# Scores of a chunked linear attention computed below the diagonal only, in quarters of the TensorE array

## The chip, the cores and the metric

The kernel runs on one core of one Trainium2 chip. The metric is the device time of one execution in microseconds (us); lower is better. TensorE is called PE below, its weight loads PEld; VectorE is DVE, ScalarE ACT, GpSimd POOL, and SyncE, which here only issues DMAs, SP.

## What is computed

A linear attention with decay (RWKV-5) runs over 4 batches, 8 heads, 768 tokens and head size 48, and its output is routed to one of 8 experts (3072 tokens of width 384, hidden width 1024):

```python
for t in range(S):
    cur = einsum('bhd,bhe->bhde', u[None] * k[:, :, t], v[:, :, t])
    y[:, :, t] = einsum('bhd,bhde->bhe', r[:, :, t], state + cur)
    state = w[None, :, :, None] * state + einsum('bhd,bhe->bhde', k[:, :, t], v[:, :, t])
...
e = argmax(x @ w_gate);  out = gate * (relu(x @ w1[e]) @ w2[e])
```

Everything is float32. Cut into chunks of 128 tokens, the attention of one chunk is a 128x128 matrix of scores between the chunk's own tokens (strictly later tokens see earlier ones, with the decay; a token sees itself through u), applied to v, plus the state of all earlier chunks.

## The kernel before

**Stages.** The attention takes 16 pairs of heads (U = 16, four pairs to each of four batches), each of 6 chunks of C = 128 tokens. Two heads of 48 channels lie in one tile, at partitions 0 to 47 and 64 to 111; 48 to 63 are zero rows that are loaded with r and k. After the attention the tokens, sent to a table of rows in HBM by indirect DMA from POOL (`send`, L410), are read back expert by expert, and two dense layers follow; that stage is not touched.

**One pair.** The loop over pairs is at L732, and the order on every engine is the order of the calls there. For pair i: PE forms the products of each token with itself, `p_own` (L279), from `rp` = r*k, which POOL's `pairs` (L270) made; DVE turns them (`own_t`, L288). PE forms the scores, `p_scores` (L291): for 6 chunks and 2 heads one product of 48 rows, 128 weight columns and 128 moving columns, the whole 128x128 square. The two heads lie in two row halves of the array. ACT writes 12 scaled identity matrices into the tile A (`diag`, L300: 12 activations), the diagonal of the scores. DVE copies the scores over it where a mask, `strict`, says so (`mask`, L305: 3 copies, which leave out what is on and above the diagonal). PE then does `p_tr(i-2)` (L356: output turned, and gate logits), `p_ds(i)` (L315: the chunks' state increments from `Kd`), and `p_out(i-1)` (L329: A times v at L340, state times r at L345). DVE's `scan` (L323) runs the state over the chunks. ACT's `keep` (L361) and `out_t` (L348) empty PSUM. DVE's `scale` (L264) multiplies r and k by decays for pair i+1, POOL's `pairs(i+1)` and `keys(i+1)` (L274, `Kd` = k times decay, one instruction of 128x480) follow; for i in 7, 8, 11, 12 `keys` goes to DVE.

**Order.** On POOL each pair begins with a copy of one element, `turn` (L744), that waits for `own_t(i)`, and so holds back `pairs(i+1)`. Once in four pairs (i = 6, 10, 14) comes the rank of the previous batch's tokens (`p_rank`, `slots`, `gates`), and once (i = 5, 9, 13) the choice of experts, `choose` (L368, six short DVE instructions). The `send`s stand at the end of a pair on POOL: one for i = 6, two for i = 7 and 8, one for i = 9, and so on. For i = 7, 11 and 15 the scores of chunks 4 and 5 come after `p_ds`. In pairs 6, 10 and 14 `mask(i, 2)` stands ahead of `keep(i-2)`.

**Start.** Before the loop: PE runs 17 filling products (L121) while the first loads arrive; the decays are made on POOL and DVE (L141); `key_decay` and `p_key_decay` (L156, L160) make the table T3 that `keys` needs: DVE product, 4 PE transposes, 2 ACT copies. Then pair 0's steps, 8 more filling products on yps[0] (L730), and pair 1.

**Data.** The first three r, k loads and all later ones are one DMA of 112 partitions (L94). v and k lie token by token in vk, chunk by chunk.

Of the kernel before, what the change touches and what calls it, by code (L numbers as in the profile page):

```python
# [40 lines left out]
def bc(ap, shape):  # L41
    return ap.to_broadcast(shape)


def straight(tc, rk, vk, w, w1, w2, out, flag):
# [45 lines left out]
    def load_rk(i):  # L91
        if i < U:
            b, hp = divmod(i, HP)
            nc.sync.dma_start(rks[i % 3][0:KP], rk[b, hp].rearrange("h p u s -> (h p) u s")[0:KP])  # L94

    def load_vk(i):
        if i < U:
# [9 lines left out]
    def p_fill(n, o):  # L107

        for _ in range(n):
            nc.tensor.matmul(o, lhsT=ident, rhs=ident, start=True, stop=True, skip_group_check=True)  # L110
# [4 lines left out]
    def clear():  # L115
# [2 lines left out]
        nc.sync.dma_start(rows.rearrange("(e n) c -> e (n c)", e=E)[:, PAD * HP * Q:CAP * HP * Q].rearrange(  # L118
            "e (p z) -> p e z", p=128), bc(zt[:, None, :], [128, E, nz]))

    p_fill(17, X01[1][:, 0, :])  # L121
    strict = cp.tile([128, C], FP32, name="strict")
    nc.gpsimd.memset(strict, 1.0)
    nc.gpsimd.affine_select(out=strict, in_=strict, pattern=[[1, C]], base=-1, channel_multiplier=-1,
                            compare_op=ALU.is_ge, fill=0.0)

    pw = cp.tile([KP, 8, HP], FP32, name="pw")
    nc.vector.tensor_scalar(out=pw[:, 0, :], in0=wt, scalar1=W_LO, scalar2=W_HI, op0=ALU.max, op1=ALU.min)
# [1 line left out]
    TTf = TT.rearrange("p a u c -> p (a u c)")  # L130
    inv = cp.tile([KP, HP], FP32, name="inv")

    T3c = cp.tile([KP, HP, C], FP32, name="T3c")
    T3 = cp.tile([128, HP, 2 * D], FP32, name="T3")

    def two(h0, nh, first, second, n):

# [16 lines left out]
                                bc(inv[:, h0:h0 + nh, None, None], [KP, nh, 2, m]), op=ALU.mult)  # L154

    def key_decay(h0, nh):  # L156
        nc.vector.tensor_tensor(T3c[:, h0:h0 + nh, :], TT[:, h0:h0 + nh, 1, :],
                                bc(pw[:, 7, h0:h0 + nh, None], [KP, nh, C]), op=ALU.mult)

    def p_key_decay(h0, nh):  # L160
        for hp in range(h0, h0 + nh):
            nc.tensor.transpose(tr[:, hp * 128:hp * 128 + KP], T3c[:, hp, :], ident[0:KP, 0:KP])
        nc.scalar.copy(T3[:, h0:h0 + nh].rearrange("p a (h d) -> p a h d", h=2),
                       tr[:, h0 * 128:(h0 + nh) * 128].rearrange("p (a h d) -> p a h d", a=nh, h=2)[:, :, :, 0:D])


    dec = cp.tile([KP, HP, D, G - 1], FP32, name="dec")
# [22 lines left out]
        nc.scalar.copy(sel[:, :, :, 2 * D:], wgs)  # L190

    def numbers():
        nc.gpsimd.tensor_copy(tri, strict)
        nc.gpsimd.memset(ones, 1.0)
        nc.gpsimd.iota(it[:, 0:E], pattern=[[-1, E]], base=E, channel_multiplier=0)
        nc.gpsimd.tensor_copy(rev, it[:, 0:E])
        nc.gpsimd.iota(it[:, E:2 * E], pattern=[[N // 128, E]], base=0, channel_multiplier=0)
        nc.gpsimd.tensor_copy(osum, it[:, E:2 * E])
# [61 lines left out]
    def place(c, h):  # L260

        return c + 4 * h if c < 4 else 8 + 2 * h + c - 4
# [10 lines left out]

    def keys(i, eng=None):  # L274
        hp, v = i % HP, vks[i % 4]
        (eng or nc.gpsimd).tensor_tensor(Kds[i % 2], v[:, G:2 * G - 1, :], bc(T3[:, hp, None, :], [128, G - 1, 2 * D]),
                                         op=ALU.mult)

    def p_own(i):  # L279


        hp = i % HP
        x = rps[i % 2][0:KP].rearrange("p (c a j) -> p a c j", a=4, j=32)
        for a in range(4):
            nc.tensor.matmul(dsb[32 * a:32 * a + 2, 240:240 + 32 * G].rearrange("p (c j) -> p c j", j=32),
                             lhsT=ubs[:, hp, :], rhs=x[:, a], start=True, stop=True, skip_group_check=True)

    def own_t(i):  # L288
        nc.vector.transpose(own[i % 2].rearrange("p c m -> p (c m)"), dsb[:, 240:240 + 32 * G])  # L289

    def p_scores(i, cs):  # L291
        r = RKs[i % 3]
        for c in cs:
            for h in range(2):
                q = slice(64 * h, 64 * h + D)
                o = X01[h][:, c, :] if c < 4 else X23[:, h, (c - 4) * C:(c - 3) * C]
                nc.tensor.matmul(o, lhsT=r[q, 1, c * C:(c + 1) * C], rhs=r[q, 0, c * C:(c + 1) * C],  # L297
                                 start=True, stop=True, skip_group_check=True)

    def diag(i):  # L300
        A = Aw[i % 2]
        for c, h in [(c, 0) for c in range(4)] + [(c, 1) for c in range(4)] + [(c, h) for h in range(2) for c in (4, 5)]:
            nc.scalar.activation(A[:, place(c, h), :], ident, func=ACT.Copy, scale=own[i % 2][:, c, h:h + 1])  # L303

    def mask(i, k):  # L305
        A = Aw[i % 2]
        m = strict.bitcast(I32)
        if k < 2:
            nc.vector.copy_predicated(A[:, 4 * k:4 * k + 4, :], bc(m[:, None, :], [128, 4, C]), X01[k])  # L309
        else:  # L310
            nc.vector.copy_predicated(A[:, 8:12, :].rearrange("p (h c) t -> p h c t", h=2),
                                      bc(m[:, None, None, :], [128, 2, 2, C]),
                                      X23[:, :, 0:2 * C].rearrange("p h (c t) -> p h c t", c=2))

    def p_ds(i):  # L315
        v = vks[i % 4]
# [640 lines left out]
def general(tc, rk, vk, w, w1, w2, out):  # L957
# [117 lines left out]
    def load_pair(b, hp):  # L1075
        i = b * HP + hp
        kT, rT = kTs[i % 2], rTs[i % 2]
        for hi in range(2):
            q = slice(64 * hi, 64 * hi + D)
            nc.sync.dma_start(rT[q, :], rk[b, hp, hi, 0:D, 0])  # L1080
            nc.sync.dma_start(kT[q, :], rk[b, hp, hi, 0:D, 1])
        vt = ap2.tile([128, G, 2 * D], FP32, name="vt")
        nc.sync.dma_start(vt, vk[b, hp][:, 0:G, :])
        return kT, rT, vt

    def half(b, hp, hf, kT, rT, vt, St, xb):
# [330 lines left out]
def _layout(inputs):  # L1417


    import numpy as _np  # L1420
    x = {k: _np.asarray(v) for k, v in inputs.items()}
    r, k, v = (x[n].reshape(B, HP, 2, S, D) for n in "rkv")
    rk = _np.zeros((B, HP, 2, 64, 2, S), _np.float32)
    rk[:, :, :, 0:D, 0] = r.transpose(0, 1, 2, 4, 3)
    rk[:, :, :, 0:D, 1] = k.transpose(0, 1, 2, 4, 3)
    vk = _np.concatenate([a.reshape(B, HP, 2, G, C, D).transpose(0, 1, 4, 3, 2, 5).reshape(B, HP, C, G, 2 * D)[:, :, :, :n]
                          for a, n in ((v, G), (k, G - 1))], axis=3)
    w = _np.ones((KP, HP), _np.float32)
# [34 lines left out]
```

## Time and profile before

| | us |
|---|---|
| median of 3 runs | 372.37 (370.84 to 372.86) |
| the profiled execution, its own time | 367.2 |
| its span | 365.3 |
| attention: pair 2's `p_own` to the first expert product (L479) | 20.0 to 110.2 |
| one pair in that stretch, `p_own` to `p_own` | 6.22; 6.62 with the rank; 6.55 with split scores |
| busy in the span: PE, DVE, POOL, ACT | 353.3, 261.5, 204.6, 142.7 |

The profile is one execution, so sums below are made against its span and then carried to the median. A row of instruction groups gives line, engine, operation, output and inputs with their shapes, count, total busy time, the mean of one in ns, and the idle time before them with its releaser. The timeline gives start, duration, engine, line, operation. In the chain of waits (the work that ended last, followed back from the end) each piece has start, length and name; the chain passes through PE almost without a break from 20.0 us on. [...] PE counts are twice the calls: x24 is 12 products. Two DMAs bring a pair: 672 KB of r, k and 528 KB of vk; from 10 to 60 us the 16 DMA engines are 93% busy or more.

### The profile page before, as it was taken

The page shows a single profiled execution, that of the slowest core. Times are in us where ns is not written, and L with a number is a line of the kernel's source. Part 1 is how long each engine was busy: PE and PEld are TensorE (multiplying, and loading weights), DVE is VectorE, ACT ScalarE, POOL GpSimd, SP SyncE. Part 2 cuts the span into 40 slices and gives each one's busy share as a digit, 9 for nine tenths or more (in the row PEclk, how much of TensorE's full clock was granted, in tenths as well). Part 3 has the DMA queues.
Part 4 walks back from the last instruction along what each step waited for, and adds up shares of the span by engine and source line. Part 5 has one row for each costly group of instructions (what it writes and reads, how often), then busy time and mean ns, then how long its engine had stood idle before and what let it go on. Part 6 is the DMA issues. An engine that isn't in the chain of part 4 may idle for free.

```text
span 365.3 us, 9077 instructions
## 1 busy us (share of the span) xinstructions
PE 353.3 (97%) x3355; PEld 335.1 (92%) x3355; DVE 261.5 (72%) x653; ACT 142.7 (39%) x411; POOL 204.6 (56%) x242
## 2 busy tenths in 40 slices
PE   8999999999999999999999999999999999999991
PEld 8788888878889999999999999999999999999891
DVE  6988798887872258675797994896788688685531
ACT  2688787777784301323213312312221231122210
POOL 5389889898864521642107308805912941999341
PEclk9999999999999999999999999999999999999998
DMA  7999999986566974988358237525842943313301
GB/s 211 272 253 241 282 255 264 255 249 195 212 170 203 316 282 99 245 257 217 126 178 196 88 92 200 159 86 168 191 129 93 210 148 127 102 51 108 126 20 50
DMA packets 35205, 65.08 MB, mean 178 GB/s; under 512 B 18617, under 2 KB 19657, under 8 KB 35152
## 3 DMA queue, kind: packets, MB, share of 16 engines
q1 hardware_dynamic: 29648, 49.86, 50.3%
q0 software_dynamic: 3776, 9.84, 7.6%
q10 hardware_dynamic: 1728, 4.72, 3.7%
q8 instruction: 28, 0.46, 0.6%
q14 instruction: 25, 0.20, 0.2%
HBM read 53.29 MB, written 11.40 MB: 177 GB/s over the span
## 4 chain that ended last, share of the span: by engine, by line
PE 90%; DVE 2%; POOL 2%; issue 2%; DMA 1%; POOLq 0%; ACT 0%; DVEq 0%
PE X L501 12%; PE X L563 10%; PE X L479 8%; PE tr L603 7%; PE yps L603 7%; PE X L297 6%; PE yps L340 6%; PE yps L501 5%; PE tr L358 5%; PE yps L345 3%; PE tr L501 3%; PE dsb L501 3%; PE dsb L603 3%; PE yps L563 2%; PE dsb L320 2%
## 5 line engine op out<-in xcount | busy, mean ns | idle before, releaser
L675 POOL DMA_INDIRECT out_dram<-yo,ix x28 | 28.4, 1013 | 68.0 <-DVE ia L592 63.8
L303 ACT ACTIVATE A<-ident,own 128x128 f32<-128x128 f32 x192 | 57.9, 390 | 7.0 <-DVE own L289 6.6
L412 POOL DMA_INDIRECT rows<-xb,slot x24 | 30.3, 1262 | 12.0 <-issue 4.8
L563 PE MATMUL X<-hT,w2s 128*128 128x160 f32 (+5 forms) x288 | 36.5, 287 | 0.0
L563 PEld LDWEIGHTS X<-hT,w2s 128*128 128x128 f32 x288 | 36.2, 191 | 0.2
L603 PE MATMUL yps<-tums,sums 128*128 128x192 f32 x184 | 32.4, 326 | 0.0
L603 PEld LDWEIGHTS yps<-tums,sums 128*128 128x128 f32 x184 | 30.3, 190 | 0.0
L675 POOL DMA_INDIRECT out_dram<-yt,it x16 | 16.8, 1048 | 22.1 <-DVE so L621 10.9
L272 POOL TENSOR_TENSOR rp<-rk 112x768 f32<-112x768 f32 x15 | 28.8, 1919 | 0.0
L266 DVE TENSOR_TENSOR RK<-rk,TT 112x1536 f32<-112x1536 f32 x16 | 27.8, 1735 | 1.1 <-DMA rk<-in_rk_dram 0.9
L297 PEld LDWEIGHTS X<-RK 48*128 48x128 f32 x384 | 23.1, 187 | 5.3 <-issue 4.3
L297 PE MATMUL X<-RK 48*128 48x128 f32 x384 | 27.1, 283 | 0.2 <-DVE RK L266 0.2
L309 DVE COPY_PREDICATED A<-strict,X 128x512 f32<-128x512 int32 x32 | 23.3, 742 | 5.0 <-ACT A L303 4.9
L501 PE MATMUL X<-xT,w1s 128*128 128x208 f32 (+5 forms) x120 | 26.0, 331 | 0.0
L689 POOL TENSOR_TENSOR tums<-w2s,tums 128x384 f32<-128x384 f32 x24 | 24.7, 1031 | 0.4
L340 PE MATMUL yps<-A,vk 128*48 128x128 f32 x384 | 24.0, 274 | 0.0
L501 PEld LDWEIGHTS X<-xT,w1s 128*128 128x128 f32 x120 | 20.9, 190 | 0.0
L340 PEld LDWEIGHTS yps<-A,vk 128*48 128x48 f32 x384 | 20.2, 123 | 0.5
L637 ACT COPY so<-tr 128x192 f32<-128x192 f32 x7 | 2.2, 318 | 44.4 <-PE tr L603 44.4
L689 DVE TENSOR_TENSOR sums<-hT 128x512 f32<-128x512 f32 x16 | 17.1, 1066 | 3.2 <-ACT hT L481 3.2
L603 PE MATMUL tr<-w2s,hT 128*128 128x192 f32 x112 | 19.4, 326 | 0.0
L530 ACT ACTIVATE hT<-hT 128x416 f32<-128x416 f32 (+5 forms) x23 | 12.3, 536 | 17.9 <-DVE hT L522 17.8
(214 smaller groups left out, 828.2 us busy)
## 6 DMA issues: line engine op xcount, KB each, us to landing
w1s<-in_w_dram SPq DMA_DIRECT2D x36, 384.0 KB, 3.2
rk<-in_rk_dram SPq DMA_DIRECT2D x16, 672.0 KB, 10.2
w2s<-in_w_dram SPq DMA_DIRECT2D x24, 384.0 KB, 3.8
vk<-in_vk_dram SPq DMA_DIRECT2D x16, 528.0 KB, 5.6
w2s<-in_w_dram ACTq DMA_DIRECT2D x8, 384.0 KB, 5.6
xs<-rows SPq DMA_DIRECT2D x16, 169.0 KB, 5.3
w1s<-in_w_dram ACTq DMA_DIRECT2D x4, 384.0 KB, 3.3
rows<-zt SPq DMA_DIRECT2D x1, 1248.0 KB, 8.9
```

The lines of the kernel that those rows point to most:

```text
L266: nc.vector.tensor_tensor(RKs[i % 3][0:KP].rearrange("p u (c t) -> p u c t", t=C), x[0:KP].rearrange("p u (c t) -> p u c t", t=C), bc(TT[: ...
L272: (eng or nc.gpsimd).tensor_tensor(rps[i % 2][0:KP], x[0:KP, 0], x[0:KP, 1], op=ALU.mult)
L297: nc.tensor.matmul(o, lhsT=r[q, 1, c * C:(c + 1) * C], rhs=r[q, 0, c * C:(c + 1) * C], start=True, stop=True, skip_group_check=True)
L303: nc.scalar.activation(A[:, place(c, h), :], ident, func=ACT.Copy, scale=own[i % 2][:, c, h:h + 1])
L340: nc.tensor.matmul(o(c, h), lhsT=v[:, c, h * D:(h + 1) * D], rhs=A[:, place(c, h), :], start=c < 2, stop=c == 0, skip_group_check=True)
L412: s_ = nc.gpsimd.indirect_dma_start(out=rows[:, :], out_offset=bass.IndirectOffsetOnAxis(ap=slot[b % 2][:, c:c + 1], axis=0), in_=xbs[b % ...
L479: nc.tensor.matmul(p[:, 0:self.n], lhsT=w1s[self.k % 2][f // 2][:, m, f % 2 * 128:(f % 2 + 1) * 128], rhs=self.t[:, m, 0:self.n], start=m ...
L501: nc.tensor.matmul(p[:, at * n:(at + 1) * n], lhsT=a, rhs=b, start=j == 0, stop=j == len(ab) - 1, skip_group_check=True)
L563: nc.tensor.matmul(p[:, 0:n], lhsT=w2s[self.k % 2][f // 2][:, f % 2, m * 128:(m + 1) * 128], rhs=self.h[:, f, self.c:self.n], start=f == 0 ...
L603: nc.tensor.matmul(p[:, at * Z:(at + 1) * Z], lhsT=a(f), rhs=b(f), start=f == 0, stop=f == FT // 2 - 1, skip_group_check=True)
L675: s_ = nc.gpsimd.indirect_dma_start(out=to[:, :], out_offset=bass.IndirectOffsetOnAxis(ap=at, axis=0), in_=x, in_offset=None, bounds_check ...
L689: (eng or nc.vector).tensor_tensor(o, a, b, op=how)
```

## The change

1. `p_scores` splits each chunk's product in two: z = 0, s in 0 to 63 (64 weight columns) against all 128 t; z = 1, s in 64 to 127 against t in 64 to 127 only. The quarter with s above and t below, all of it above the diagonal, is not formed. 24 products replace 12. The output half of z is `64 * (z ^ (c & 1))`: in odd chunks the halves of s are swapped, so that four consecutive products lie in four quarters of the array (2 row halves for the heads, 2 column halves).
2. Everything that is laid out by s follows the swap in odd chunks: the rows of vk (swapped on the host), the mask (`strict` becomes [128, 2, 128]), the identity for `diag` (`eyes`, two forms), `p_own` (8 products of 96 moving columns in place of 4 of 192), T3 (a second, rotated form for each pair of heads: 8 transposes and 4 ACT copies in place of 4 and 2), and `keys` (two instructions, 128x288 and 128x192, in place of one of 128x480).
3. r, k loads from pair 3 on: two DMAs of 48 partitions in place of one of 112, without the zero rows.
4. The 17 filling products are spread over all score banks.

```diff
     def load_rk(i):
...
+            if i < 3:
+                nc.sync.dma_start(rks[i % 3][0:KP], rk[b, hp].rearrange("h p u s -> (h p) u s")[0:KP])
+            else:
+                for h in range(2):
+                    nc.sync.dma_start(rks[i % 3][64 * h:64 * h + D], rk[b, hp, h, 0:D])
...
+    strict = cp.tile([128, 2, C], FP32, name="strict")
     nc.gpsimd.memset(strict, 1.0)
+    for q, par, base in ((slice(0, 128), 0, -1), (slice(0, 64), 1, -65), (slice(64, 128), 1, -1)):
+        nc.gpsimd.affine_select(out=strict[q, par, :], in_=strict[q, par, :], pattern=[[1, C]], base=base,
+                                channel_multiplier=-1, compare_op=ALU.is_ge, fill=0.0)
+    eyes = cp.tile([128, 2, C], FP32, name="eyes")
+    for par in range(2):
+        for k in range(2):
+            nc.gpsimd.tensor_copy(eyes[:, par, 64 * k:64 * k + 64], ident[:, 64 * (k ^ par):64 * (k ^ par) + 64])
...
     def key_decay(h0, nh):
+        nc.vector.tensor_tensor(T3c[:, h0:h0 + nh, 0:C], TT[:, h0:h0 + nh, 1, :],
                                 bc(pw[:, 7, h0:h0 + nh, None], [KP, nh, C]), op=ALU.mult)
+        nc.gpsimd.tensor_copy(T3c[:, h0:h0 + nh, C:], T3c[:, h0:h0 + nh, 0:64])

     def p_key_decay(h0, nh):
         for hp in range(h0, h0 + nh):
+            o = (tr[:, 0:256], tr[:, 256:512], yps[0][:, 0:256], yps[1][:, 0:256])[hp]
+            for par in range(2):
+                nc.tensor.transpose(o[:, par * 128:par * 128 + KP], T3c[:, hp, 64 * par:64 * par + C], ident[0:KP, 0:KP])
+            nc.scalar.copy(T3[:, hp].rearrange("p u (h d) -> p u h d", h=2),
+                           o.rearrange("p (u h d) -> p u h d", u=2, h=2)[:, :, :, 0:D])
...
     def keys(i, eng=None):
         hp, v = i % HP, vks[i % 4]
-        (eng or nc.gpsimd).tensor_tensor(Kds[i % 2], v[:, G:2 * G - 1, :], bc(T3[:, hp, None, :], [128, G - 1, 2 * D]),
-                                         op=ALU.mult)
+        for par in range(2):
+            (eng or nc.gpsimd).tensor_tensor(Kds[i % 2][:, par::2, :], v[:, G + par:2 * G - 1:2, :],
+                                             bc(T3[:, hp, par:par + 1, :], [128, G // 2 - par, 2 * D]), op=ALU.mult)

     def p_own(i):
...
+        for par in range(2):
+            for a in range(4):
+                p = 32 * (a ^ (2 * par))
+                nc.tensor.matmul(dsb[p:p + 2, 240:240 + 32 * G].rearrange("p (c j) -> p c j", j=32)[:, par::2],
+                                 lhsT=ubs[:, hp, :], rhs=x[:, a, par::2], start=True, stop=True, skip_group_check=True)
...
     def p_scores(i, cs):
         r = RKs[i % 3]
-        for c in cs:
-            for h in range(2):
-                q = slice(64 * h, 64 * h + D)
-                o = X01[h][:, c, :] if c < 4 else X23[:, h, (c - 4) * C:(c - 3) * C]
-                nc.tensor.matmul(o, lhsT=r[q, 1, c * C:(c + 1) * C], rhs=r[q, 0, c * C:(c + 1) * C],
+        for c0 in cs[::2]:
+            for z, c, h in [(z, c0 + (z ^ x), h) for z in range(2) for x in range(2) for h in range(2)]:
+                q, p = slice(64 * h, 64 * h + D), 64 * (z ^ (c & 1))
+                o = X01[h][p:p + 64, c, 64 * z:C] if c < 4 else X23[p:p + 64, h, (c - 4) * C + 64 * z:(c - 3) * C]
+                nc.tensor.matmul(o, lhsT=r[q, 1, c * C + 64 * z:c * C + 64 * z + 64], rhs=r[q, 0, c * C + 64 * z:(c + 1) * C],
                                  start=True, stop=True, skip_group_check=True)
...
-            nc.scalar.activation(A[:, place(c, h), :], ident, func=ACT.Copy, scale=own[i % 2][:, c, h:h + 1])
+            nc.scalar.activation(A[:, place(c, h), :], eyes[:, c & 1, :], func=ACT.Copy, scale=own[i % 2][:, c, h:h + 1])
```

`mask` still makes three copies of 128x512, with the doubled mask. The order of the calls in the loop is as before.

More of the change, by code (lines that the diff above doesn't have):

```diff
@@ L93, in load_rk @@
             b, hp = divmod(i, HP)
-            nc.sync.dma_start(rks[i % 3][0:KP], rk[b, hp].rearrange("h p u s -> (h p) u s")[0:KP])
+            if i < 3:
[3 more added lines that the diff above has]
+                    nc.sync.dma_start(rks[i % 3][64 * h:64 * h + D], rk[b, hp, h, 0:D])
     def load_vk(i):
@@ L119, in clear @@
             "e (p z) -> p e z", p=128), bc(zt[:, None, :], [128, E, nz]))
-    p_fill(17, X01[1][:, 0, :])
-    strict = cp.tile([128, C], FP32, name="strict")
+    for k in range(12):
+        p_fill(1 + (k < 5), X01[k // 4][:, k % 4, :] if k < 8 else X23[:, k % 2, (k - 8) // 2 * C:(k - 6) // 2 * C])
+    strict = cp.tile([128, 2, C], FP32, name="strict")
     nc.gpsimd.memset(strict, 1.0)
-    nc.gpsimd.affine_select(out=strict, in_=strict, pattern=[[1, C]], base=-1, channel_multiplier=-1,
-                            compare_op=ALU.is_ge, fill=0.0)
+    for q, par, base in ((slice(0, 128), 0, -1), (slice(0, 64), 1, -65), (slice(64, 128), 1, -1)):
[5 more added lines that the diff above has]
+            nc.gpsimd.tensor_copy(eyes[:, par, 64 * k:64 * k + 64], ident[:, 64 * (k ^ par):64 * (k ^ par) + 64])
     pw = cp.tile([KP, 8, HP], FP32, name="pw")
@@ L131, in straight @@
     inv = cp.tile([KP, HP], FP32, name="inv")
-    T3c = cp.tile([KP, HP, C], FP32, name="T3c")
-    T3 = cp.tile([128, HP, 2 * D], FP32, name="T3")
+    T3c = ca.tile([KP, HP, C + 64], FP32, name="T3c")
+    T3 = cp.tile([128, HP, 2, 2 * D], FP32, name="T3")
     def two(h0, nh, first, second, n):
@@ L156, in key_decay @@
     def key_decay(h0, nh):
-        nc.vector.tensor_tensor(T3c[:, h0:h0 + nh, :], TT[:, h0:h0 + nh, 1, :],
+        nc.vector.tensor_tensor(T3c[:, h0:h0 + nh, 0:C], TT[:, h0:h0 + nh, 1, :],
                                 bc(pw[:, 7, h0:h0 + nh, None], [KP, nh, C]), op=ALU.mult)
+        nc.gpsimd.tensor_copy(T3c[:, h0:h0 + nh, C:], T3c[:, h0:h0 + nh, 0:64])
     def p_key_decay(h0, nh):
         for hp in range(h0, h0 + nh):
-            nc.tensor.transpose(tr[:, hp * 128:hp * 128 + KP], T3c[:, hp, :], ident[0:KP, 0:KP])
-        nc.scalar.copy(T3[:, h0:h0 + nh].rearrange("p a (h d) -> p a h d", h=2),
-                       tr[:, h0 * 128:(h0 + nh) * 128].rearrange("p (a h d) -> p a h d", a=nh, h=2)[:, :, :, 0:D])
+            o = (tr[:, 0:256], tr[:, 256:512], yps[0][:, 0:256], yps[1][:, 0:256])[hp]
[3 more added lines that the diff above has]
+                           o.rearrange("p (u h d) -> p u h d", u=2, h=2)[:, :, :, 0:D])
     dec = cp.tile([KP, HP, D, G - 1], FP32, name="dec")
@@ L192, in numbers @@
     def numbers():
-        nc.gpsimd.tensor_copy(tri, strict)
+        nc.gpsimd.tensor_copy(tri, strict[:, 0, :])
         nc.gpsimd.memset(ones, 1.0)
@@ L283, in p_own @@
         x = rps[i % 2][0:KP].rearrange("p (c a j) -> p a c j", a=4, j=32)
-        for a in range(4):
-            nc.tensor.matmul(dsb[32 * a:32 * a + 2, 240:240 + 32 * G].rearrange("p (c j) -> p c j", j=32),
-                             lhsT=ubs[:, hp, :], rhs=x[:, a], start=True, stop=True, skip_group_check=True)
+        for par in range(2):
[3 more added lines that the diff above has]
+                                 lhsT=ubs[:, hp, :], rhs=x[:, a, par::2], start=True, stop=True, skip_group_check=True)
     def own_t(i):
@@ L302, in diag @@
         for c, h in [(c, 0) for c in range(4)] + [(c, 1) for c in range(4)] + [(c, h) for h in range(2) for c in (4, 5)]:
-            nc.scalar.activation(A[:, place(c, h), :], ident, func=ACT.Copy, scale=own[i % 2][:, c, h:h + 1])
+            nc.scalar.activation(A[:, place(c, h), :], eyes[:, c & 1, :], func=ACT.Copy, scale=own[i % 2][:, c, h:h + 1])
     def mask(i, k):
         A = Aw[i % 2]
[L307 to L313, printed above, removed]
+        m = bc(strict.rearrange("p u t -> p (u t)").bitcast(I32)[:, None, :], [128, 2, 2 * C])
+        o = A[:, 4 * k:4 * k + 4, :].rearrange("p (z c) t -> p z (c t)", z=2)
+        nc.vector.copy_predicated(o, m, X01[k].rearrange("p (z c) t -> p z (c t)", z=2) if k < 2 else X23[:, :, 0:2 * C])
     def p_ds(i):
@@ L1082, in load_pair @@
         vt = ap2.tile([128, G, 2 * D], FP32, name="vt")
-        nc.sync.dma_start(vt, vk[b, hp][:, 0:G, :])
+        nc.sync.dma_start(vt[:, 0::2], vk[b, hp][:, 0:G:2, :])
+        for k in range(2):
+            nc.sync.dma_start(vt[64 * k:64 * k + 64, 1::2], vk[b, hp][64 - 64 * k:128 - 64 * k, 1:G:2, :])
         return kT, rT, vt
@@ L1427, in _layout @@
                           for a, n in ((v, G), (k, G - 1))], axis=3)
+    for c in [c for c in range(2 * G - 1) if c % G % 2]:
+        vk[:, :, :, c] = _np.roll(vk[:, :, :, c], C // 2, axis=2)
     w = _np.ones((KP, HP), _np.float32)
```

## Prediction

> **What bounds the kernel now.** I read the page's busy shares first (PE 97%), then the chain of waits in order of time. From 20 us on it is PE, one step after another; this is one whole pair (start, length, engine, output, line, instructions):
>
> ```profile
> 26.29 0.44 PE dsb L285 x8
> 26.73 1.54 PE X L297 x24
> 28.27 1.07 PE tr L358 x8
> 29.34 0.45 PE X L358 x4
> 29.78 0.58 PE dsb L320 x20
> 30.37 1.31 PE yps L340 x24
> 31.68 0.83 PE yps L345 x20
> ```
>
> The sum is 6.22 us; the scores (L297) are 1.54 of it. But a PE that never idles can stand beside engines that hardly do. So I then read the timelines of ACT, DVE and POOL. Around the rank (pair 5's `own_t` to pair 7's):
>
> ```profile
> 39.30 0.38 DVE L289 STREAM_TRANSPOSE own<-dsb 128x192 f32<-128x192 f32 x1 [0.73 <-PE dsb L285]
> 46.36 0.38 DVE L289 STREAM_TRANSPOSE own<-dsb 128x192 f32<-128x192 f32 x1
> 46.83 3.62 ACT L303 ACTIVATE A<-ident,own 128x128 f32<-128x128 f32 x12 [0.91 <-DVE own L289]
> 51.65 0.33 ACT L364 COPY xb<-X 128x208 f32<-128x208 f32 x1 [0.82 <-DVE se L399]
> 51.88 0.86 ACT L350 COPY yT<-yps 112x384 f32<-112x384 f32 x2
> ```
>
> No PE stands in the brackets after 39.30: ACT's 12 diagonals, DVE's masks, `choose`, the next diagonals, masks, `keep` and `out_t` follow one another for 13.44 us, to 52.74. PE's `p_tr(5)` needs that `out_t` and starts at 53.09. **PE is ahead of a second chain by only 0.35 us there.** POOL in pair 8:
>
> ```profile
> 59.24 2.88 POOL L412 DMA_INDIRECT rows<-xb,slot  x1 [0.30 <-DVE own L289]
> 62.12 0.18 POOL L744 COPY turn<-own 1x1 f32<-1x1 f32 x1
> 62.27 1.82 POOL L272 TENSOR_TENSOR rp<-rk 112x768 f32<-112x768 f32 x1
> ```
>
> `rp` ends at 64.09, and PE's `p_own` that reads it starts at 64.26. A third chain, 0.2 us behind. The start, pairs 0 and 1:
>
> ```profile
> 12.66 2.05 PE L110 MATMUL yps<-ident 128*128 128x128 f32 x16
> 13.24 1.82 POOL L272 TENSOR_TENSOR rp<-rk 112x768 f32<-112x768 f32 x1
> 14.10 0.38 ACT L163 COPY T<-tr 128x288 f32<-128x288 f32 x1
> ```
>
> Here PE waits for POOL (`p_own(1)` at 15.12), and its fills are cover.
>
> [...] the 48x48 products of L345 lie in four quarters, and start in fours at 69.64, 69.83, 69.94 and 70.05, one four per 109 ns. [...] a send takes 0.98 us alone and 2.88 across `scale` (58.99 to 60.71) and `keys` on DVE (to 61.27). [...] L297, 128 columns, goes in twos per 111.5 ns [...].
>
> **Part 1, scores on PE.** L297 is 12 groups of two x 111.5 = 1.34, plus 0.20 at its ends. After: three chunk pairs, each two passes of four 64x128 products and two of four 64x64. The first group costs 109 as L345 does (128 moving columns). The second: L320 (48 columns loaded, 48 moved) goes in twos per 45 ns, [...]. 6 x 109 + 6 x 58 = 1.00, plus 0.19 (L345's ends: 0.83 - 6 x 0.109 = 0.18) = 1.19. **Saving 0.35 a pair.** [...] I take 0.35, as L345's fours load within 109 and L320's halves within 45.
>
> `p_own`: 16 instructions of 96 columns for 8 of 192. Two groups at 162 become four at about 82: no change [...]. Masks and diagonals: same shapes, nothing.
>
> **Part 2, `keys` in two.** POOL's 480 elements take 1.20, 768 take 1.82: 2.15 ns an element and 0.17 fixed. So +0.17 on POOL a pair; on DVE (0.65, 0.95) +0.15. On POOL it lies behind `rp` in cover (1 us or more until the next `own_t`); on DVE (pairs 7, 8, 11, 12) it stands ahead of the send, `turn` and `rp` [...], in the third chain: +0.15 each. Cover gone, POOL's would cost 0.17 a pair.
>
> **Part 3, loads.** 576 KB for 672, one more issue on SP (0.32, SP idle most of the pair). No scores wait for these DMAs now, so the gain is 0; bounds 0 to -0.3 in pair 10, where ACT waits 2.0 for a send's landing among them.
>
> **Part 4, start.** Before `decays`, POOL gets two more selects (0.27 each), a longer memset (0.1) and four copies (0.2 each, near L193's 0.28 for twice the size): 1.4, of which 1.04 is its idle time; the 0.4 left is covered, as `scale(0)` waits for its load until 6.80 (0.93). Then T3's rotated form: POOL copies 256 elements after DVE's T3c (10.04), to 10.5; transpose; ACT's T3 to 11.15 (10.68 before); `keys(0)` in two to 11.9, `scale(1)` to 13.65 (13.04). Behind the copy on POOL now stand `state_decay`'s memset and copy (1.7 us), done by 6.8 before; [...] `scan(0)` moves from 12.96 to 14.55, `pairs(1)` ends near 16.8 (15.06). And PE: two T3 forms now pass through yps[0] and yps[1]; the 8 fills write yps[0], so they wait for ACT's copy, which stands behind pair 0's diagonals: 11.05 + 3.52 + two copies = 15.1. Fills 15.15 to 17.2, **`p_own(1)` at 17.2 for 15.12**. From there as before (own, `scale(2)`, `turn`, `rp`): `p_own(2)` at 22.0 for 20.0. **Cost +2.0**; bounds +0.8 (copies and fills in half the time) and +3.
>
> **The sum.** Pairs 2 to 4 are PE's alone: 3 x -0.35 = -1.0. Pairs 5 to 7: PE would need 14.36 - 0.70 - 0.23 = 13.43 from `p_own(5)` to `p_tr(5)`, the second chain gives 0.57 + 13.44 + 0.05 = 14.06: only -0.3 of 0.93. Pairs 7, 8: third chain, `own_t` to `rp` 5.41 + 0.15, with `p_own` and `own_t` 6.2: about +0.1. Pairs 9 to 11: ACT already makes PE wait (0.55 at 79.23, for a send's landing [...]): -0.1, and -0.1 to the end of pair 11. Pair 12: -0.35. Pairs 13 to 15: as 5 to 7, -0.3, and -0.1. Together +2.0 - 1.0 - 0.3 + 0.1 - 0.2 - 0.35 - 0.4 = **-0.15**. The experts' stage follows unmoved. The profiled execution took 367.2 (span 365.3), 5.2 below the median of the runs; the difference is carried to the median: 372.2.
>
> **Rivals.** *A, forecast: no change*, 372.2, own range 370.5 to 374: 0.53. *B, faster: PE remains the bound.* If the second and third chain are looser than their rows look (a wait is put down to the releaser that came last, and engines that nothing presses may simply trail), 14 pairs x 0.35 = -4.9, and +2.0: 369.5; with half the start's cost 368.5. For it: PE at 97%, no long PE wait but one. Against: the brackets above. 0.27. *C, slower: column halves load one after the other.* From 112 ns a group on nothing is saved, and the start's +2.0 and `keys`' +0.4 remain: 374.8; if all four loads follow one another, [...]. Against: L345, L320. 0.20. That the change doesn't do what it says: the smaller loads are hidden anyway, as counted.
>
> A measurement of this kernel tells about 0.5% (1.9 us) from no change. B lies over it, most of A within, C over. The range 368.3 to 375.2 takes in A, B and the first form of C.
>
> **What would show it.** Right: L318 x48 in 1.2 us a pair, `p_own(2)` near 22, PE waits before `p_tr` in pairs 7, 11, 15 on ACT's yT, and in pairs 8, 9 on POOL's `rp`. Wrong: PE without waits and a pair at 5.9 throughout (B); L318 at 1.5 or more (C); `p_own(2)` near 20.

## The result, and the profile after

| | before | after |
|---|---|---|
| median, us | 371.88 (370.84 to 372.86, 4 runs) | 382.71 (380.63 to 384.69, 4 runs) |
| ratio, 95% interval | | 1.029 (1.023 to 1.036) |
| the profiled execution / its span, us | 367.2 / 365.3 | 384.69 / 382.9 |
| start: `p_own(2)` at | 20.0 | 23.8 |
| loop: `p_own(2)` to the first expert product | 90.1 | 100.4 |
| the experts' stage, to the end | 255.2 | 258.7 |

Slower by 2.9%, outside the range. 10.3 of the 17.6 us between the two spans arise in the loop, 3.8 at the start, 3.5 after it. (Before's profiled execution lies 4.7 us under its median, so not all of the 17.6 is the change's.) A ratio, here and below, leaves out executions that fell in a slower state; a median takes in all.

Page rows: busy time with the number of instructions, the granted clock in 40 slices, the queue that carries instructions (packets, MB, share). First the kernel before:

```profile
PE 353.3 (97%) x3355; PEld 335.1 (92%) x3355; DVE 261.5 (72%) x653; ACT 142.7 (39%) x411; POOL 204.6 (56%) x242
...
PEclk9999999999999999999999999999999999999998
...
q8 instruction: 28, 0.46, 0.6%
```

The kernel after:

```profile
PE 360.1 (94%) x3871; PEld 341.5 (89%) x3871; DVE 262.2 (68%) x658; ACT 143.4 (37%) x413; POOL 209.1 (55%) x260
...
PEclk9699996999699999999999999999999999999998
...
q8 instruction: 32, 0.52, 0.6%
```

PE got 516 products and 516 weight loads more: with both counted as records, 280 a pair for 216. Its clock, 9 in all slices but the last before, has three dips.

The chain of waits of the kernel after, two stretches of the loop (start, length, what; "issue" is time in which nothing that the profile shows was waited for):

```profile
29.72 0.44 PE dsb L304 x16
30.17 1.16 PE X L318 x48
31.33 1.07 PE tr L375 x8
32.40 0.45 PE X L375 x4
32.84 0.58 PE dsb L337 x20
33.43 1.31 PE yps L357 x24
34.74 0.83 PE yps L362 x20
...
48.42 0.47 PE X L318 x11
48.90 1.32 issue
50.21 1.00 PE X L318 x27
...
55.86 0.27 PE dsb L304 x7
56.13 2.42 issue
58.55 0.41 PE dsb L304 x9
58.96 1.28 PE X L318 x32
60.25 1.96 PE tr L375 x8
62.21 0.85 PE X L375 x4
```

The pair at 29.72 is what was forecast: 5.85 us, the scores 1.16 (1.54 before). Then PE stops twice in the middle of one step (11 of 48, 7 of 16) and waits for no engine. After the longer stop the same eight transposes take 1.96 for 1.07. The same in windows (busy time and count by engine, clock, DMA share, GB/s):

```profile
22.00:48.00 26.00, 25.23 (x595) 21.85 (x593) 20.90 (x28) 21.91 (x71) 22.93 (x28) 1.00 0.76 210
48.00:59.00 11.00, 7.26 (x167) 5.97 (x168) 7.04 (x18) 6.15 (x19) 8.23 (x20) 1.00 1.02 235
59.00:68.00 9.00, 9.00 (x140) 8.06 (x140) 5.32 (x8) 4.76 (x16) 6.04 (x4) 0.62 0.37 111
...
98.00:106.00 8.00, 8.00 (x124) 7.17 (x123) 3.59 (x9) 3.20 (x10) 4.55 (x4) 0.65 0.57 154
```

The stops lie where the DMA engines are full (1.02); the low clock follows. Lost by the clock: 0.38 x 9 + 0.35 x 8 = 6.2 us. The second of these two stretches has no long stop ahead of it, only 1.1 us in which PE idles: 0.71 us of waiting for `rp`, up to 94.66, and a short stop:

```profile
94.66 0.51 PE dsb L304 x16
...
95.28 1.07 PE X L318 x33
96.35 0.40 issue
96.75 0.71 PE X L318 x3
```

The start of the kernel after, PE and then ACT in the timeline:

```profile
15.72 3.22 PE L115 MATMUL yps<-ident 128*128 128x128 f32 x16 [0.36 <-ACT T L179]
18.87 0.51 PE L304 MATMUL dsb<-rp,wug 112*2 112x96 f32 x16
```

```profile
11.64 3.61 ACT L324 ACTIVATE A<-eyes,own 128x128 f32<-128x128 f32 x12
15.16 0.30 ACT L179 COPY T<-tr 128x192 f32<-128x192 f32 x1
```

The 8 fills wait for ACT's copies of T3, which stand behind 12 diagonals: the mechanism that was forecast (fills at 15.15). But the clock is 6 tenths in this slice, so they take 3.22 us where 2.05 was taken, and `p_own(1)` is at 18.87 (17.2 forecast).

### The profile page after: what moved, and what is told of

It is laid out like the page before. It is cut to its first block, busy times and chain, and to the rows that moved or that the text cites. A ratio compares the mean times of both kernels' runs of the same rounds, so it can differ in the third digit from the quotient of the medians.

```text
span 382.9 us, 10165 instructions
## 1 busy us (share of the span) xinstructions
PE 360.1 (94%) x3871; PEld 341.5 (89%) x3871; DVE 262.2 (68%) x658; ACT 143.4 (37%) x413; POOL 209.1 (55%) x260
## 4 chain that ended last, share of the span: by engine, by line
PE 80%; ACT 6%; DVE 6%; issue 3%; DMA 2%; POOL 1%; another core or an unknown queue 1%; POOLq 0%; SPq 0%; DVEq 0%; ACTq 0%
PE X L518 12%; PE X L580 9%; PE X L496 8%; PE tr L620 7%; PE yps L620 7%; ACT A L324 5%; PE yps L518 5%; PE yps L357 4%; PE X L318 4%; PE tr L375 4%; PE tr L518 3%; PE dsb L518 3%; PE dsb L620 3%; PE yps L580 2%; PE yps L362 2%
## 5 line engine op out<-in xcount | busy, mean ns | idle before, releaser
L324 ACT ACTIVATE A<-eyes,own 128x128 f32<-128x128 f32 x192 | 57.9, 389 | 13.7 <-DVE own L308 12.4
L330 DVE COPY_PREDICATED A<-strict,X 128x512 f32<-128x512 int32 x48 | 34.7, 735 | 9.8 <-ACT A L324 4.6
L429 POOL DMA_INDIRECT rows<-xb,slot x24 | 24.2, 1007 | 12.6 <-issue 5.1
L318 PE MATMUL X<-RK 48*64 48x128 f32 (+1 forms) x768 | 25.9, 264 | 5.1 <-issue 2.7
L318 PEld LDWEIGHTS X<-RK 48*64 48x64 f32 x768 | 21.1, 142 | 9.8 <-issue 6.9
L761 POOL COPY turn<-own 1x1 f32<-1x1 f32 x14 | 20.6, 1472 | 14.1 <-DVE own L308 13.9
L288 POOL TENSOR_TENSOR rp<-rk 112x768 f32<-112x768 f32 x15 | 27.3, 1817 | 0.0
L375 PE MATMUL tr<-sel,yT 112*128 112x104 f32 x128 | 20.7, 307 | 1.2 <-issue 1.0
L375 PEld LDWEIGHTS tr<-sel,yT 112*128 112x128 f32 x128 | 17.4, 208 | 3.2 <-issue 1.5
L367 ACT COPY yT<-yps 112x384 f32<-112x384 f32 x32 | 13.8, 481 | 16.3 <-PE yps L362 8.3
```

The source lines that it names most:

```text
L288: (eng or nc.gpsimd).tensor_tensor(rps[i % 2][0:KP], x[0:KP, 0], x[0:KP, 1], op=ALU.mult)
L318: nc.tensor.matmul(o, lhsT=r[q, 1, c * C + 64 * z:c * C + 64 * z + 64], rhs=r[q, 0, c * C + 64 * z:(c + 1) * C], start=True, stop=True, sk ...
L324: nc.scalar.activation(A[:, place(c, h), :], eyes[:, c & 1, :], func=ACT.Copy, scale=own[i % 2][:, c, h:h + 1])
L330: nc.vector.copy_predicated(o, m, X01[k].rearrange("p (z c) t -> p z (c t)", z=2) if k < 2 else X23[:, :, 0:2 * C])
L375: nc.tensor.matmul(trv[c // 4][:, c % 4, :], lhsT=yTs[i % 3][0:KP, c & 1, (c // 2) * C:(c // 2 + 1) * C], rhs=sel[:, c & 1, i % HP, :], st ...
```

## Where PE stops: a regularity in the trace

Count PE's records (products, weight loads and the few that wait for semaphores) from zero, in order of their starts. The two long stops in the loop of the kernel after, and a shorter one, come ahead of record 193 + 256 n: ahead of 1217 (0.50 us from start to start), 1729 (1.53), 1985 (2.67). An instruction packet is 0.52 MB / 32 = 16 KB, and the kernel after has 4 more of them (32 for 28) for 1032 more records of PE: about 258 records to a packet, near the 256 between the stops. So 256 records of PE are called a block here; that each packet brings the next block is inferred from these counts and from the times below. Times of the packets, from the trace:

```
              block entered  next block's packet starts  PE goes on   stop
before            21.1              25.8                   28.8       none
before            43.2              46.4                   50.5       none
before            50.5              51.4                   57.7       none
after             43.1              47.6                   50.2       1.53
after             50.2              55.6                   58.5       2.67
```

A packet starts up to 5.4 us after the block before it was entered, and at each stop PE goes on 2.5 to 2.9 us after that start. Such delays are there in the kernel before too (4.7 us in the first row), without a stop. A block lasts 7.0 to 8.3 us in the kernel before and, at the full clock and where nothing stops it, 4.4 to 6.1 in the kernel after. Delay and fetch together, by an estimate from the table some 3 to 8 us (0.9 + 2.5 to 5.4 + 2.9), were covered by the longer block and are not always by the shorter one.

Theories for the experiments. **F**: TensorE starves for instructions, as there are more of them in less time, and the stops bring the clock down. (The table shows packets that start late; that they wait behind data in the DMA engines is part of the theory.) **D**: r, k in two DMAs made the DMA engines slower. **S**: the start, the other engines' chains and the clock by itself. Chips differ in the level of the kernel before (366.65 to 371.88 us), so each run is given as a ratio to the kernel before on its own chip.

## Experiments

**1. One r, k DMA again, in the kernel after.**

```diff
-            if i < 3:
-                nc.sync.dma_start(rks[i % 3][0:KP], ...)
-            else:
-                for h in range(2):
-                    nc.sync.dma_start(rks[i % 3][64 * h:64 * h + D], rk[b, hp, h, 0:D])
+            nc.sync.dma_start(rks[i % 3][0:KP], rk[b, hp].rearrange("h p u s -> (h p) u s")[0:KP])
```

> The changed kernel with part 3 undone: r and k of a pair in one DMA of 112 partitions again, everything else as changed. Theory F (PE runs out of instructions: a pair now has 280 PE records for 216, they are fetched in blocks of 256, a block lasts 5.4 to 5.9 us for 7.3, and the fetch stands in the DMA engines behind the data): the bytes rise by 96 KB a pair, so the gaps on PE stay or grow: 381 to 387 us. Rival D (the two DMAs of 48 partitions are what delays the fetches or the loads): the gaps shrink, 374 to 378 us. Rival S (the start, and the waits between ACT, DVE and POOL with the clock that falls after them, without fetches): no difference, 382 to 384.

Measured: 381.0, ratio 1.022 (1.013 to 1.032). The long stop ahead of record 1985 is there again (2.29 us), so D falls as the main cause. That it has a small share is not excluded: the interval begins inside the range that D gave (374 to 378 us, up to 1.016).

**2. The kernel before with as many PE instructions as after.**

```diff
     def p_own(i):
...
+        for n in range(16):
+            a = n % 4
+            nc.tensor.matmul(dsb[32 * a:32 * a + 2, 240:241], lhsT=ubs[:, hp, :], rhs=rps[i % 2][0:KP, 0:1],
+                             start=True, stop=True, skip_group_check=True)
```

> The kernel before, with 16 one-column products ahead of pair's p_own (64 more PE records a pair, 280 in all; their output is overwritten). Theory F: gaps on PE that nothing in the trace explains, at multiples of 256 records, as in the changed kernel, 3 us or more in all, and a lower clock after the longest: 377 to 386 us. Rivals D and S: no such gaps; only the products' own time, 0.1 to 0.4 us a pair: 373 to 378 us.

Measured: 386.8, ratio 1.043 (1.036 to 1.050). Nothing of the change is in this kernel but the count of 280. PE's timeline in it:

```profile
55.38 0.24 PE L286 MATMUL dsb<-rp,wug 112*2 112x1 f32 x11
56.86 0.28 PE L286 MATMUL dsb<-rp,wug 112*2 112x1 f32 x19 [1.24 <-issue]
```

This stop (1.40 between records) is ahead of record 1985, as after; others are ahead of 449, 705 and 1729 (0.85, 1.12 and 0.43), 3.8 us in all. But six more, of 0.4 to 0.7 us, lie inside blocks, in pairs 8 to 14 (3.5 us; 6 has more of this sort), and the clock, which is at half for 6.8 us from 67.0 and again from 97.7, falls right behind two of these each time (0.65 and 0.66 us ahead of 64.3 and 65.0), not behind the long one. The kernel before has no stop of either sort. The added products themselves last 0.2 to 0.3 us a pair, so a part of the 15.8 us, at most 16 x 0.3 = 5, is their work.

**3. The kernel after with `p_own` in 4 products of 192 columns** (the swap is in the access pattern of the moving operand): 264 records a pair.

```diff
+        x = rps[i % 2][0:KP]
+        for a in range(4):
+            rhs = bass.AP(x.tensor, x.offset + 32 * a, [list(x.ap[0]), [2 * C, G // 2], [192 if a < 2 else 64, 2], [1, 32]])
+            nc.tensor.matmul(dsb[32 * a:32 * a + 2, 240:240 + 32 * G].rearrange("p (c u j) -> p c u j", u=2, j=32),
+                             lhsT=ubs[:, hp, :], rhs=rhs, start=True, stop=True, skip_group_check=True)
```

> The changed kernel with p_own in 4 products of 192 columns for 8 of 96 (the swap of odd chunks put into the moving operand's pattern): 264 PE records a pair for 280. Theory F: a block lasts 6% longer; gaps get shorter by 0.3 us each where they stand: 378 to 382 us. Rivals D and S: the same time as the changed kernel, 382 to 384.

Measured: 375.8, ratio 1.011 (1.004 to 1.018), beside 1.022 (1.013 to 1.032) for experiment 1 on the same chip: shorter, though the two intervals meet. The pair is as short as with 280 (5.84 us where nothing stops it), the stops ahead of 1729 and 1985 are 1.28 and 1.76 us. These are no shorter in sum than those in the profile of experiment 1 (2.29 and 0.21); what is shorter is the time at half clock in the loop, 6.8 us for 17.1. So this gain agrees with F but is not seen to come from shorter stops.

**4. The r, k load of pair i+4 issued in the middle of pair i.**

```diff
-        load_rk(i + 3)
+        if i == 1:
+            load_rk(4)
...
+        load_rk(i + 4)
         load_vk(i + 3)
```

> The changed kernel with the load of r, k issued half a pair apart from that of v, k (behind pairs(i+1), so in the middle of a pair) instead of right behind it; same bytes, same DMAs. Theory F: the burst that a fetch can stand behind is half as long, most unexplained gaps on PE go: 374 to 378 us. Rival D: shorter too, but less. Rival S: no PE step waits for these loads, so nothing: 382 to 384, or slower if scale comes to wait for its load.

Measured: 380.0, ratio 1.025 (1.018 to 1.032). A miss: when the loads start matters little, the stops ahead of 1729 and 1985 remain.

**5 and 6. Both kernels without the later loads** (and without the fallback for a full expert). The edit is the same in both.

```diff
     def load_rk(i):
-        if i < U:
+        if i < 3:
...
     def load_vk(i):
-        if i < U:
+        if i < 4:
```

> The kernel before without the loads of r, k from pair 3 on and of v, k from pair 4 on (the pairs then work on the data of earlier pairs), and without the fallback path that the tokens' counts could call; all else as it was. A reference for the next one. Theory F (PE starves for instructions, whose fetch stands behind data in the DMA engines): the kernel before just hides its fetches, so little changes: 366 to 371 us, a pair 6.2 us. Rival S (chains and clock): the same.

> The changed kernel with the same loads and the fallback left out. Theory F: fetches come within 1 us of their request, no unexplained gap on PE, a pair 5.85 where no chain binds, and the start's +3.8 us remains: 365 to 372 us, within 1% of the run without loads of the kernel before. Rival S (the start, waits between ACT, DVE and POOL, the clock): these are still there: 378 us or more.

Measured: before 369.0, ratio 0.991 (0.989 to 0.994); after 376.2, ratio 1.011 (1.007 to 1.015); between the two 1.02. In the kernel after a packet now starts within 1.5 us of its block's entry, from the second pair on (the block of record 1729: entered at 48.97, next packet at 50.09, passed at 54.94), and no stop lies ahead of a block any more. But it is still 7 us slower than the kernel before: the stops ahead of blocks are not the whole loss. A part of the rest is PE's waits for `rp` (1.1 us in pair 8, 1.0 in pair 12); another is a second sort of stop, about 0.55 us each, eight in all (4.3 us), in pairs 8 to 14 only:

```profile
62.60 1.29 PE L318 MATMUL X<-RK 48*64 48x128 f32 x35
64.22 0.59 PE L318 MATMUL X<-RK 48*64 48x128 f32 x13 [0.33 <-issue]
```

They begin 0 to 0.9 us after the start of an indirect send of POOL's (here at 63.60), not at a block. See 11 and 13.

**7. The fills first:** 24 fills at once and the other 8 ahead of `p_key_decay`.

```diff
-        p_fill(1 + (k < 5), X01[k // 4]...)
+        p_fill(2, X01[k // 4]...)
...
+    p_fill(8, yps[0][:, 384:512])
     p_key_decay(1, 3)
```

> The changed kernel with its start mended: 24 filling products for 17 (in the changed kernel they end 2.2 us before the first scores), and the 8 fills on yps[0] ahead of the transposes of T3 for pairs 1 to 3, so that they don't wait for ACT. p_own(2) then starts near 21 for 23.8. Theory F: the start is a cost of its own, and the rest shifts with it: 379 to 381 us. Rival S in its strong form (the start and the clock's fall there are most of the loss): 374 to 377. If later waits absorb it: 382 to 384.

Measured: 386.9, ratio 1.042 (1.036 to 1.048). The start gains 1.3 us (`p_own(2)` at 22.5 for 23.8; near 21 was expected), and the run loses more: the steps meet the blocks at other times, with stops of 1.26 at 24.2 and of 2.85 at 60.5. The start was not most of what made the change slow.

**8. The clearing of the rows in 8 DMAs,** two a pair in pairs 1 to 4, for one of 1248 KB, issued at 41.7 us in the kernel after, ahead of the two long stops.

```diff
...
-        if i == 4:
-            clear()
+        if i < 5:
+            clear(range(2 * i - 2, 2 * i))
```

> The changed kernel with the 1248 KB that clear rows in HBM sent in 8 DMAs, two in each of pairs 1 to 4, in place of one in pair 4. Theory F, with these writes as the queue that the fetches near 47 and 55 us stand in: the two longest unexplained gaps (1.5 and 2.7 us) and the fall of the clock after the second (3.3 us) go: 375 to 379 us. If the queue there is of other data, or the pieces make gaps earlier: 381 to 385. Rival S: 382 to 384.

Measured: 381.1, ratio 1.025 (1.021 to 1.029). The stops without a cause fall from 7.7 us to about 4, those at 48 and 56 are gone, and the time hardly falls: stops of the second sort remain, others are ahead of records 1217 and 2241 (0.76 and 0.65), and the clock drops again in pair 8, which takes 9.95 us.

**9. As 3, and the even chunks' scores in one 128x128 product again:** 240 records.

```diff
+            for h in range(2):
+                ...
+                nc.tensor.matmul(o, lhsT=r[q, 1, c0 * C:(c0 + 1) * C], rhs=r[q, 0, c0 * C:(c0 + 1) * C],
+                                 start=True, stop=True, skip_group_check=True)
+            for z, c, h in [(z, c0 + 1, h) for z in range(2) for h in range(2)]:
```

> The changed kernel with the decay products in four of 192 columns, as in the run before it, and with the even chunks' scores in one product of 128 x 128 again (their halves are not swapped, so that is the old form); only the odd chunks are in parts: 240 PE records a pair for 264 and 280. The scores' stretch gets longer, by up to 0.2 us a pair. F (TensorE starves for instructions): each block of 256 records lasts longer again, 6.3 us and more, so fewer or shorter gaps at records 193 + 256 n: ratio to the kernel before 0.998 to 1.008, below the 1.011 of 264 records. S (the start and the chains of the other engines set it): these are as they were, and the scores cost more: 1.011 to 1.02.

Measured: 381.8, ratio 1.039 (1.037 to 1.042). The time is missed by far, by a cost not thought of. One pair's scores in PE's timeline:

```profile
32.21 0.49 PE L317 MATMUL X<-RK 48*128 48x128 f32 x4
32.63 0.44 PE L322 MATMUL X<-RK 48*64 48x128 f32 x8
33.00 0.49 PE L317 MATMUL X<-RK 48*128 48x128 f32 x4
33.42 0.43 PE L322 MATMUL X<-RK 48*64 48x128 f32 x8
33.79 0.49 PE L317 MATMUL X<-RK 48*128 48x128 f32 x4
34.21 0.44 PE L322 MATMUL X<-RK 48*64 48x128 f32 x8
34.58 0.69 PE L379 MATMUL tr<-sel,yT 112*128 112x104 f32 x4
```

From 32.21 to 34.58 is 2.37 us, where quarters alone take 1.16 and halves alone 1.54: groups of 4 and 8 alternate, and by these times each change of form costs: 2.37 less half of 1.16 + 1.54 leaves 1.02 us for five changes, by estimate 0.2 us each. The pair is 7.04. On F the trace does speak: blocks last 7.2 us and more, and this kernel has no stop at all, of either sort, and no dip of the clock in the loop. As both a lower count and slower work lengthen a block, that agrees with F and does not single out the count.

**10. Experiments 3 and 8 together; then 7 as well.** No new edit.

> The changed kernel with the decay products in four of 192 columns (264 records a pair), and with the clearing of the rows in 8 transfers, two a pair in pairs 1 to 4, in place of one after pair 4: both together, and the start as the change has it. F: the long gaps at records 1729 and 1985, which 264 records alone still showed, go, as they went where the clearing was spread with 280 records, and the clock does not fall after them: 1.000 to 1.008. S: as with 264 records alone, 1.011.

> As the kernel with four decay products and the spread clearing, and with the start's fills in the order that let the second pair begin earlier (24 first fills of equal number, and the other 8 ahead of the transposes of the key decays): the candidate to beat both. F: the fills no longer coincide with a stall, so the 1 to 2 us that the start gained stay: 0.993 to 1.003. S (the start cost 2 to 4 us of the loss): 0.998 to 1.006. If the early fills bring the clock down, as it seemed where they were moved alone, it is above the kernel without them, 1.005 to 1.02.

Measured: 369.0, ratio 1.0058 (1.0034 to 1.0082); and 369.6, ratio 1.0054 (1.0031 to 1.0077), against 366.65. Most of the loss is gone (2.9%, or 2.1% in 12 on another chip), with the change's scores as they were. The second one's profile has the clock of before in every slice and a loop of 88.5 us; its start is at 22.4. Its page row:

```profile
PEclk9999999999999999999999999999999999999997
```

Stops ahead of blocks are fewer and shorter here, not gone: 0.47, 0.72, 0.36 and 0.97 us in this loop, 1.07 in that of the first and 1.56 ahead of it; those at records 1729 and 1985 are in neither. This execution (367.5) is 2 us below the median of its runs. S fell short here: with the fills first the start gains 1.2 us and the total nothing.

**11. As 6, with each pair's sends issued one pair later,** between POOL's `pairs` and `keys`, past the scores' beginning.

```diff
             pairs(i + 1)
+            if i - 1 in sends:
+                send(*sends[i - 1])
             keys(i + 1, ...)
...
-        if i in sends:
-            send(*sends[i])
+        if i == U - 1:
+            for j in (i - 1, i):
+                send(*sends[j])
```

G stands for: a send beside the dense scores halts PE.

> The changed kernel without the loads of r, k from pair 3, of v, k from pair 4 and without the fallback for a full expert (so later pairs work on old data), as the run of that kind before it, and with each pair's indirect sends issued one pair later between GpSimd's products for the decays and those for the keys, some 3 us after the scores of a pair begin in place of at their beginning. G (GpSimd's work for an indirect send halts TensorE where its records are dense): the gaps of 0.5 to 0.6 us in the scores, eight of them, 4.3 us in all, go, and the pairs from 8 on are shorter by 0.5 us each: 372 to 374 us for 376.2. The rival (the gaps have another cause, or the pairs there are set by GpSimd's decays for the next pair anyway): the gaps stay, or go with no gain, 375.5 to 378.

Measured: 378.5, ratio 1.033 (1.029 to 1.037). The eight stops are gone and most pairs are at 5.85; but the last send of a batch now holds the buffer that `keep` writes: PE waits 1.7 us on yT at 81.0, and 5.7 at 109.8, where that send had itself waited 3.9 us for a load of weights.

**12. The kernel before with the clearing spread; the kernel after once more,** on one chip with the next two.

> The kernel before with the clearing of the rows in 8 transfers, two a pair in pairs 1 to 4. F: its blocks of 256 records last 7.0 to 7.9 us, no fetch is late, so there is nothing to win: 0.997 to 1.003. If the clearing costs the kernel before as well (data queued ahead of its loads), 0.99 to 0.995, and the recovery of the changed kernel by the same edit says less about the change.

> The changed kernel as it is, beside the others of this set on one chip. If the chip sets only the level: 1.026 to 1.032 of the kernel before, as first measured. If a chip on which the kernel before runs 5 us faster also delays fetches less (F's size is in the DMA engines' delays, which may differ by chip): 1.01 to 1.025.

Measured: 367.3, ratio 0.9991 (0.9963 to 1.0019); and 375.9, ratio 1.021 (1.016 to 1.025). The kernel before gains nothing, so whatever the spread clearing gave back in 10 was the change's own loss. The kernel after had its long stops again ahead of records 1729 (1.26) and 1985 (3.22), with three shorter ones (0.21, 0.21, 0.60) 5.5 us ahead of blocks, and no stop of the second sort. Its clock is at half for 10.2 us behind the longest, 5.1 us lost. Its loop is 6.6 us longer than that of the kernel before with the clearing spread, so on this chip F's stops and the clock behind them are enough for the loss. It is smaller than on the first chip, though the two intervals meet.

**13. Only the six sends moved that hold nothing up** (of pairs 6 to 8 and 10 to 12): without loads, and in the best version of 10.

```diff
+            if i - 1 in (6, 7, 8, 10, 11, 12):
+                send(*sends[i - 1])
...
-        if i in sends:
+        if i in sends and i not in (6, 7, 8, 10, 11, 12):
```

> The changed kernel without the loads of r, k from pair 3, of v, k from pair 4 and without the fallback, with the indirect sends of pairs 6, 7, 8 and 10, 11, 12 issued one pair later between GpSimd's products for the decays and those for the keys; those of pairs 9, 13, 14, 15 stay, as a buffer or the end of the loop waits for them. G (a send beside the dense scores halts TensorE): gaps in the scores only after pairs 9 and 13 to 15, none elsewhere, and the pairs without a gap at 5.9 to 6.3 us for 6.8 to 7.2: 372 to 374.5 us, or 0.99 to 0.995 of the run without loads that left the sends where they were. The rival (GpSimd's decays set those pairs anyway): gaps gone, time as before within 0.5 us.

> The best version so far (four decay products, clearing in 8 parts, fills in the other order) with the same six sends moved by a pair. That version's profile shows no gaps beside the sends, so by G there is nothing to gain: 1.002 to 1.008 of the kernel before, as without the move. If it becomes faster by over 0.5%, the sends cost in another way (they hold GpSimd back from the next pair's decays).

Measured: 367.6, ratio 0.9994 (0.9965 to 1.0022); and 371.8, ratio 1.007 (1.004 to 1.010). The second is on the chip of 12, where the kernel after is at 1.021 (1.016 to 1.025): two thirds of that loss are gone. Its profile, from its longest execution (376.8), still has six stops of 0.5 to 1.8 us ahead of blocks and a clock that falls behind the longest two, so the fetch remains close. The first seemed to prove G: no stop, a loop of 88.5 us. To take the chip out, the run without loads was made again on one chip, with the sends in place and with six moved:

> The changed kernel without the loads of r, k from pair 3, of v, k from pair 4 and without the fallback, beside the same with six sends moved, on one chip. G: 1.1% or some 4 us above it, with gaps in the scores beside the sends. The rival (the chip made the difference of the two first runs): within 0.3% of it.

> The same with six sends issued one pair later. G: 0.986 to 0.992 of the run with the sends in place, no gaps in the scores. The rival: within 0.3% of it.

Measured: 374.9, ratio 1.0083 (1.0057 to 1.011), and 372.9, ratio 1.0033 (1.0012 to 1.0053): 372.87 / 374.89 = 0.995, between the two expectations. And the stops were back. The same kernel twice, PE and POOL of pair 9; first the run with none:

```profile
65.43 1.23 PE L318 MATMUL X<-RK 48*64 48x128 f32 x48
```

```profile
64.47 1.01 POOL L429 DMA_INDIRECT rows<-xb,slot  x1 [0.16 <-issue]
65.78 0.97 POOL L429 DMA_INDIRECT rows<-xb,slot  x1 [0.30 <-issue]
```

And the last run:

```profile
65.50 0.93 PE L318 MATMUL X<-RK 48*64 48x128 f32 x18
66.69 0.45 PE L318 MATMUL X<-RK 48*64 48x128 f32 x5 [0.26 <-issue]
67.41 0.74 PE L318 MATMUL X<-RK 48*64 48x128 f32 x25 [0.27 <-issue]
```

```profile
64.81 1.01 POOL L429 DMA_INDIRECT rows<-xb,slot  x1 [0.16 <-issue]
66.12 0.97 POOL L429 DMA_INDIRECT rows<-xb,slot  x1 [0.30 <-issue]
```

In both a send falls into the scores; in one PE stops twice, in the other not. So G is too simple: the stops come during or just after sends, but a send does not by itself bring one. What decides it stays open. The 2.0 us that the move did save can be seen in part: PE's wait of 1.15 us for `rp` in pair 8 is gone.

No version beat the kernel before.

## Why the prediction was wrong

**What failed.** The step is Part 1. It priced the scores and `p_own` ("16 instructions of 96 columns for 8 of 192 ... no change") by what the array takes for them, and gave the 64 more instructions a pair no price. The diff shows the count, and the page shows the packets of q8; the sum had no term for them, and no rival was built on them. The runs put this in its place, in the loop of the profiled execution: stops ahead of instruction blocks (4.7 us), a falling clock (6.2) and stops near sends (3.0). With the -2.15 forecast for the loop that makes +11.8; +10.3 came, presumably as some of the stops cover waits that were there. (Of the 3.5 us after the loop, stops near sends, of 0.4, 0.6 and 0.8 us, are about a half; the rest is not explained.)

That F is a cause is shown from four sides: the stops lie at the blocks, 2.4 to 3.2 us after a packet's start, in every profile that has them; the count alone brings them to the kernel before (2); without the loads packets start early and these stops go, with the count unchanged (6); and fewer instructions with thinner traffic (fills and six sends moved as well) bring back two thirds of the loss on one chip (13), where the traffic alone gives the kernel before nothing (12). How large its share is on the first chip is not shown: the stops near sends and the low clock behind them cost about as much there, and their cause is open. They too come with the denser instructions, as the added products of 2 bring them to the kernel before.

That idle time of PE brings the clock down is the order in each trace, not a separate test. It falls behind every stop above 2.4 us in the loop (after, 4, 7, 12), but also behind less: 1.1 us of idle in the kernel after at 96.7, two stops of 0.65 and 0.66 in 2; 1.3 us at 50 did not do it. In the kernel after each of the two falls in the loop is to a clock of 0.50 and lasts 6.8 us.

**What was right.** The scores: 1.16 us a pair for 1.19 forecast, 1.54 before; rival C is refuted by this row alone. The 58 ns in the forecast is an estimate that two groups of the kernel before give: L320's twos take 45 ns with 48 columns loaded and L297's 111.5 with 128, and 64 columns lie on that line at 58. The pair: 5.85 where 6.22 - 0.35 = 5.87 was worked out. Loads: one DMA or two makes no great difference (1). The start's mechanism (fills behind ACT's copy of T3); its size, +2.0, came as +3.8 against before's profile, in which the clock does not fall at the start. Where it does not, the changed kernel has `p_own(2)` at 22.5 to 22.8 (8, 13), 2.5 to 2.8 later than 20.0; where it does, the kernel before too is at 22.6 to 23.6 (12, 5), and the kernel after at 23.8 to 24.9. So about one of the 3.8 us is the clock's. That `p_own(2)` follows `p_own(1)` by 4.9 us, near the 4.8 forecast, is luck: PE waits at its end for `scan`, behind ACT's diagonals and a mask, not for `rp`. `scan(0)`'s 14.55 was the author's estimate; it came at 14.72, and the copy on POOL ahead of it (L196) had ended at 12.92.

**The loop's other terms** are best read from the first run of 13, which has no stops (no loads either), against the rows of before. Pairs 2 to 4: -1.1 (-1.0 forecast). Pairs 5 to 7: -0.6 (-0.3): the second chain holds pair 6 at 6.59, but lets pair 5 go. Pair 8: -0.4 (+0.1, with 7); where the sends are not moved pair 7 takes 7.32 for 6.55, +0.8, as PE waits 1.1 us for `rp`: the third chain, and undersized: its +0.15 was the author's estimate. Pairs 9 to 11: -0.2 (-0.2). Pair 12: -0.4 (-0.35). Pairs 13 to 15: +1.0 (-0.4); PE waits there 0.5 for the new state and 1.2 for its next step, which the moved sends bring. In sum -1.7 for -2.15. The best version of 10 comes out 1.6 shorter in the loop and 2.4 later at the start in its profile: rival A's balance, in an execution whose instructions arrive nearly in time.

## What to carry to other kernels

A kernel whose TensorE is 97% busy with short products is also a stream of instructions: before splitting products, count the instructions per microsecond and compare how long 256 of them (a block here) last with how late the instruction packets start beside the kernel's own DMAs (0.9 to 5.4 us in the table), plus the time from there until PE goes on (2.4 to 3.2 us at the stops here). If the new time is near or under that sum, the split can cost more than the array time that it saves, as it did here; fewer and larger products (here an access pattern that does the swap, 16 instructions saved) and a thinner transfer at that place gave most of it back. When a profile shows "issue" in the middle of a step, count records up to it before looking for an engine to blame.

## What the runs showed of the hardware that was not expected

- 16 KB instruction packets began up to 6.0 us after their predecessor was entered while large DMAs ran (experiment 4; 5.4 in the kernel after, with a DMA share of 1.02), within 1.5 us in the loop of 6, without loads; at the stops PE went on 2.4 to 3.2 us after the start.
- A stop can be followed by a larger loss in the clock: 2.67 us of stop, then 9 us at 0.62 (3.4 us lost). So can 1.1 us of idle time in two pieces: 8 us at 0.65 (2.8 us lost).
- Alternating products of 128 weight columns with products of 64 on the array is slower than either: 2.37 us for a mixture, 1.54 and 1.16 for the pure forms.
- One kernel's stops near sends came and went between two runs on two chips (none, and 7 of together 3.4 us). The level of the kernel before differs by chip (366.65 to 371.88).
